# A chunked retention ahead of two MLPs: state matmuls on quarters of the array, query scaling on GpSimd, and an earlier second weight fetch

## Chip, cores and metric

The kernel runs on one core of a Trainium2 chip. The metric is the device time of one execution in microseconds. The trace is one profiled execution of the same kernel.

## The reference

For each batch b (2) and head h (8), over 768 positions of 64 features, a linear attention with a decay per head is computed, then two MLPs on the 1536 tokens of 512 features:

```python
for each block:                      # 64 positions in the reference
    intra = (q k^T * lam^(i-j), i>=j) v
    inter = (q * lam^(i+1)) @ state
    out   = intra + inter
    state = lam^block * state + (k * lam^(block-1-j))^T v
x = out as (tokens, heads*64)
x = relu(x @ w_in)^2 @ w_out         # 512 -> 2048 -> 512
y = leaky_relu(x @ w_in2) @ w_out2   # 512 -> 2048 -> 512
```

The weights come as float64, the rest as float32.

## The kernel before

**Retention.** The work is cut into 12 units (2 batches x 6 chunks of 128 positions), all 8 heads in one unit. A feature block of 128 partitions holds a pair of heads (p = 0 to 3), the even head in partitions 0 to 63 and the odd one in 64 to 127 (par = 0, 1). `load` (L196) fetches q, k or v of a unit, 256 KB each, on SP's queue. `transposes` (L288) turns k and q by TensorE (L294) and copies them out by ScalarE (L298). `scale_q` (L301) multiplies the transposed queries by the powers of lam, on VectorE, out of PSUM (L304). `scores` (L306) multiplies keys and queries, each head on one half of the array's rows (L311), and `mask` (L313) multiplies by the decay table (L316, VectorE). `state` (L323) scales k by GpSimd (`kd`, L329), multiplies it with v (L335), scales the old state by GpSimd (`tmp`, L342, once for each half of the partitions) and adds on VectorE (L347, or L349 in a chunk 0, twice also). The carried state `st` is a tile of 128 x 4 x 128 in which each pair's two 64 x 64 blocks stand on the diagonal and the rest is zero (L321), so that a state matmul reads 128 rows. `output` (L351) makes for each pair two state matmuls (L360, where the chunk isn't the first) and two score matmuls (L362) into one bank; `split` (L67) writes the result as a rounded part `xhi` (ScalarE, L68) and a rest `xlo` (VectorE, L69). A matmul in plain float32 stands in the trace as two MATMUL instructions, so 8 matmuls are x16.

**Order.** PE's and SP's orders in the retention are those of the program (`manual_schedule`, L414). In iteration i (L391 to L410) PE does transposes(i+2), state(i), output(i), scores(i+2), and SP issues k and q of unit i+4, v of unit i+2, and, for i = 1 and 9, a `fetch` of 1 MB of weights. VectorE, ScalarE and GpSimd work in the order that a planner gave them, except that the steps of a weight conversion in the retention are kept in program order (`pin`). k has 5 buffers, q and v 3 each, PSUM 8 banks.

**Weights.** `order` (L79) lists 32 pieces of 1 MB. `fetch` (L90) loads the next into one of two `raw` buffers; `converting` (L98) turns float64 words into a rounded and a rest part: one ScalarE pass (L114), then VectorE steps L115, L116, L118, L121, L122, L125 and, after a ScalarE copy (L135), L137. Each call of `convert` (L153) does one such step. After the step of L122 the raw tile isn't read again, and there a new fetch is made, but only if the MLP has begun:

```python
        yield ve.scalar_tensor_tensor(out=rf, in0=w_lo, ...)   # L122
        if begun_mlp:
            fetch()
```

In the retention `convert` is called once in each of the iterations 3 to 9, seven steps: the first piece.

**MLPs.** From L749 on PE's order is again the program's: first the halves of w_in against the three token tiles (first half of the first stage, then the second), then w_out, stage by stage; all MLP matmuls stand in line 503. One fetch is made at the start (L750), the others after L122.

## Time and profile before

| | us |
|---|---|
| median of 3 runs (lowest, highest) | 576.50 (575.89, 577.19) |
| the profiled execution | 576.09 |
| its span in the trace | 574.3 |
| TensorE busy in the span | 564.1 |
| VectorE busy | 418.9 |
| ScalarE busy | 304.4 |
| GpSimd busy | 90.7 |
| granted TensorE clock, share of full speed | 1.0 |

A row of a timeline gives start and length in us, the engine, the line, and the names of the tiles written and read; x4 means four instructions merged into one row; in brackets stand the idle time before it and what ended it. SPq is SP's queue of DMA issues: its time is the issuing, not the transfer. A group's row gives busy us, mean ns of one instruction, and the idle time before. PEld is TensorE's weight load.

### The profile page before, as it was taken

To read this page: it belongs to the slowest core of one execution; us is meant where nothing else is said; L and a number is where in the kernel's file an instruction comes from. 1 tells how busy PE (TensorE), PEld (TensorE's weight loads), DVE (VectorE), ACT (ScalarE), POOL (GpSimd) and SP (SyncE) were. 2 spreads that over 40 slices of the span, in tenths; PEclk is the share of its full clock that TensorE was granted. 3 is DMA by queue.
4 is the path that set the end of the run, shared out by engine and by line. 5 is a ranking of instruction groups with operands and counts; after the bars stand their busy time and mean duration, and the time that the engine had idled before them with its cause. 6 is when DMAs were issued, how large, how long until landed. Compare 5 with 4: busy or idle time off the path is not lost.

```text
span 574.3 us, 8060 instructions
## 1 busy us (share of the span) xinstructions
PE 564.1 (98%) x3075; PEld 470.4 (82%) x3075; DVE 418.9 (73%) x589; ACT 304.4 (53%) x477; POOL 90.7 (16%) x105
## 2 busy tenths in 40 slices
PE   7989999999999999999999999999999999999997
PEld 6879888888788888888888888888888888888886
DVE  3789999999927699498478999929883996217222
ACT  2344598547757587758447375453562376225110
POOL 3426000000044604343000000000213011310000
PEclk9999999999999999999999999999999999999999
DMA  8998434655498958999313215342529523661432
GB/s 173 244 201 188 155 121 135 233 184 190 163 156 138 155 175 183 211 258 227 128 36 95 80 33 218 130 164 74 105 53 246 110 33 42 76 89 56 164 111 91
DMA packets 79350, 80.75 MB, mean 141 GB/s; under 512 B 40264, under 2 KB 51792, under 8 KB 79312
## 3 DMA queue, kind: packets, MB, share of 16 engines
q1 hardware_dynamic: 61312, 62.15, 35.5%
q0 software_dynamic: 17472, 17.83, 22.9%
q8 instruction: 24, 0.39, 0.3%
q10 hardware_dynamic: 528, 0.26, 0.2%
q14 instruction: 14, 0.11, 0.1%
HBM read 55.05 MB, written 30.42 MB: 149 GB/s over the span
## 4 chain that ended last, share of the span: by engine, by line
PE 75%; DVE 16%; DMA 5%; issue 3%; ACT 1%; DVEq 0%; SPq 0%; ACTq 0%
PE ps L503 72%; DVE hb L118 2%; DVE rb L122 2%; DVE hb L125 2%; DMA v<-in_v 2%; DVE Pm L316 1%; DVE rb L121 1%; DVE hb L115 1%; DMA raw<-in_moe_w_in 1%; DVE xlo L69 1%; DMA raw<-in_moe_w_out 1%; DMA DTr<-tab 1%; DVE w2l L137 1%; PE ps L360 1%; DVE st L347 1%
## 5 line engine op out<-in xcount | busy, mean ns | idle before, releaser
L503 PE MATMUL ps<-xhi,w1h 128*128 128x512 f32 x288 | 112.2, 389 | 0.0
L503 PE MATMUL ps<-xhi,w1l 128*128 128x512 f32 x288 | 112.0, 389 | 0.0
L503 PE MATMUL ps<-xlo,w1h 128*128 128x512 f32 x288 | 112.0, 389 | 0.0
L616 POOL DMA_DIRECT2D spill<-f x48 | 47.9, 1215 | 349.9 <-ACT f L612 349.8
L612 ACT COPY f<-ps 128x512 f32<-128x512 f32 x84 | 48.7, 585 | 71.7 <-PE ps L503 71.2
L503 PEld LDWEIGHTS ps<-xhi,w1h 128*128 128x128 f32 x288 | 54.1, 188 | 11.4 <-issue 0.2
L503 PEld LDWEIGHTS ps<-xhi,w1l 128*128 128x128 f32 x288 | 54.1, 188 | 11.3
L503 PEld LDWEIGHTS ps<-xlo,w1h 128*128 128x128 f32 x288 | 54.1, 188 | 11.2
L474 DVE TENSOR_TENSOR g0l<-f,g0h 128x512 fp32r<-128x512 f32 x52 | 35.1, 687 | 32.5 <-ACT f L470 20.9
L503 PE MATMUL ps<-w2l,g0h 128*128 128x512 f32 (+1 forms) x132 | 50.5, 383 | 0.0
L503 PE MATMUL ps<-w2h,g0l 128*128 128x512 f32 (+1 forms) x132 | 50.5, 383 | 0.0
L503 PE MATMUL ps<-w2h,g0h 128*128 128x512 f32 (+1 forms) x132 | 50.5, 383 | 0.0
L137 DVE TENSOR_TENSOR w2l<-hb,w2h 128x1024 fp32r<-128x1024 f32 x16 | 19.5, 1222 | 39.8 <-ACT w2h L135 39.8
L114 ACT ACTIVATE hb<-raw 128x1024 f32<-128x1024 f32 x32 | 36.8, 1148 | 20.5 <-DVE w2l L137 7.5
L503 PE MATMUL ps<-g0h,w2h 128*128 128x512 f32 x104 | 40.5, 389 | 0.0
L503 PE MATMUL ps<-g0l,w2h 128*128 128x512 f32 x104 | 40.5, 389 | 0.0
L503 PE MATMUL ps<-g0h,w2l 128*128 128x512 f32 x104 | 40.5, 389 | 0.0
L122 DVE SCALAR_TENSOR_TENSOR rb<-raw,rb 128x1024 f32<-128x1024 uint32 x32 | 39.1, 1221 | 0.4
L125 DVE TENSOR_TENSOR hb<-hb,rb 128x1024 f32<-128x1024 f32 x32 | 39.1, 1221 | 0.4
L118 DVE SCALAR_TENSOR_TENSOR hb<-raw,hb 128x1024 uint32<-128x1024 uint32 x32 | 39.1, 1221 | 0.3
L567 DVE TENSOR_TENSOR f<-ps,f 128x512 f32<-128x512 f32 x40 | 26.2, 684 | 9.9 <-PE ps L503 9.9
L716 DVE TENSOR_TENSOR f<-ps,f 128x512 f32<-128x512 f32 (+1 forms) x25 | 16.7, 668 | 22.8 <-PE ps L503 22.8
(143 smaller groups left out, 1141.9 us busy)
## 6 DMA issues: line engine op xcount, KB each, us to landing
raw<-in_moe_w_in SPq DMA_DIRECT2D x16, 1024.0 KB, 5.6
raw<-in_moe_w_out SPq DMA_DIRECT2D x16, 1024.0 KB, 5.2
spill<-f POOLq DMA_DIRECT2D x48, 256.0 KB, 6.1
spill<-f SPq DMA_DIRECT2D x24, 256.0 KB, 2.8
f<-spill SPq DMA_DIRECT2D x24, 256.0 KB, 2.9
k<-in_k SPq DMA_DIRECT2D x12, 256.0 KB, 4.7
q<-in_q SPq DMA_DIRECT2D x12, 256.0 KB, 5.2
v<-in_v SPq DMA_DIRECT2D x12, 256.0 KB, 4.9
```

What stands on the lines that cost most here:

```text
L69: nc.vector.tensor_tensor(out=lo, in0=src, in1=hi, op=ALU.subtract)
L114: nc.scalar.activation(hf, w_hi.bitcast(F32), AF.Abs)
L118: yield ve.scalar_tensor_tensor(out=hb, in0=w_hi, scalar=0xC0000000, in1=hb, op0=ALU.bitwise_and, op1=ALU.bitwise_or)
L122: yield ve.scalar_tensor_tensor(out=rf, in0=w_lo, scalar=2.0 ** -52, in1=rf, op0=ALU.mult, op1=ALU.mult)
L125: yield ve.tensor_tensor(out=hf, in0=hf, in1=rf, op=ALU.add)
L137: yield ve.tensor_tensor(out=lo, in0=hf, in1=hi, op=ALU.subtract)
L474: nc.vector.tensor_tensor(out=glo, in0=r, in1=ghi, op=ALU.subtract)
L503: nc.tensor.matmul(ps, a, b, start=start and n == 0, stop=stop and n == len(ops) - 1, skip_group_check=again)
L567: ve.tensor_tensor(out=out, in0=ps[h, where], in1=other, op=ALU.add)
L612: nc.scalar.copy(f, src)
L616: nc.gpsimd.dma_start(dst, f, accum_op=ALU.add)
L716: nc.vector.tensor_tensor(out=a, in0=ps, in1=a, op=ALU.add)
```

## The change

The state tile has 64 columns instead of 128, without the zero blocks, and the two halves of its update become one instruction each. A state matmul takes 64 rows and writes 64 partitions. For odd pairs p the two heads change places in the output's partitions, so that four successive state matmuls lie on the four quarters of the array; output takes two banks, even pairs in one and odd pairs in the other, and is split in two instructions of each kind. All state matmuls of a unit come before its score matmuls. Because the heads of odd pairs are swapped in x, the rows of the first MLP's w_in are swapped as they are fetched: such a fetch is three DMAs (512 KB, 256 KB, 256 KB). Query scaling goes to GpSimd, from the copied queries in SBUF. The second fetch is made in iteration 6 instead of 9, and `convert` is called once in the iterations 3 to 5 and twice in 6 to 10: 13 calls.

```diff
--- before.py
+++ after.py
@@ -76,6 +76,9 @@
             return w[:, s * FS + h * CW:s * FS + (h + 1) * CW].rearrange("(k p) f -> p k f", p=P)
         return w[s * FS + h * CW:s * FS + (h + 1) * CW, :].rearrange("(k p) f -> p k f", p=P)
 
+
+    half = [slice(e * D, (e + 1) * D) for e in range(2)]
+
     order = [(0, 0, 0, 0), (0, 0, 0, 1), (0, 0, 1, 0), (0, 0, 1, 1)]
     stages = [(l, s) for l in range(2) for s in range(NS)]
     for before, stage in zip(stages, stages[1:]):
@@ -92,7 +95,13 @@
             key = todo.pop(0)
             r = raw.tile([P, 4 * CW], I64, tag="raw", name="raw")
             k = 4 if key[2] == 0 else 2
-            dma(r.rearrange("p (k f) -> p k f", k=k), source(*key))
+            dst, src = r.rearrange("p (k f) -> p k f", k=k), source(*key)
+            if key[0] or key[2]:
+                dma(dst, src)
+            else:
+                dma(dst[:, 0:k:2], src[:, 0:k:2])
+                for a, b in ((half[0], half[1]), (half[1], half[0])):
+                    dma(dst[a, 1:k:2], src[b, 1:k:2])
             fetched.append((key, r))
 
     def converting():
@@ -301,7 +310,7 @@
         def scale_q(i, ps):
             if units[i][1]:
                 qS[i] = tr.tile([P, NP, C], F32, tag="qS", name="qS")
-                ve.tensor_tensor(out=qS[i], in0=ps, in1=LR, op=ALU.mult)
+                nc.gpsimd.tensor_tensor(out=qS[i], in0=qT[i], in1=LR, op=ALU.mult)
 
         def scores(i):
             raw_scores[i] = [bank().rearrange("p (a s) -> p a s", a=NP) for _ in range(2)]
@@ -317,8 +326,7 @@
 
         st = []
         for e in range(2):
-            st.append(att.tile([P, NP, P], F32, name=f"st{e}"))
-            nc.gpsimd.memset(st[e], 0.0)
+            st.append(att.tile([P, NP, D], F32, name=f"st{e}"))
 
         def state(n):
             b, c = units[n]
@@ -337,33 +345,32 @@
             old, new = st[c % 2], st[(c + 1) % 2]
             if c:
                 tmp = wk.tile([P, NP, D], F32, tag="tmp", name="tmp")
-                for par in range(2):
-                    r = slice(par * D, (par + 1) * D)
-                    nc.gpsimd.tensor_tensor(out=tmp[r], in0=old[r, :, r],
-                                            in1=LR[r, :, C - 1:C].to_broadcast([D, NP, D]), op=ALU.mult)
-            for par in range(2):
-                r = slice(par * D, (par + 1) * D)
-                if c:
-                    nc.vector.tensor_tensor(out=new[r, :, r], in0=ps[r], in1=tmp[r], op=ALU.add)
-                else:
-                    nc.vector.tensor_copy(new[r, :, r], ps[r])
+                nc.gpsimd.tensor_tensor(out=tmp, in0=old, in1=LR[:, :, C - 1:C].to_broadcast([P, NP, D]), op=ALU.mult)
+                nc.vector.tensor_tensor(out=new, in0=ps, in1=tmp, op=ALU.add)
+            else:
+                nc.vector.tensor_copy(new, ps)
 
         def output(n):
             b, c = units[n]
             vn = nats[n, "v"]
-            ps = bank().rearrange("p (a s) -> p a s", a=NP)
-            for p in range(NP):
-
-                rows = [slice(par * D, (par + 1) * D) for par in range(2)]
-                if c:
-                    for r in rows:
-                        nc.tensor.matmul(ps[r, p, :], st[c % 2][:, p, r], qS[n][:, p, :], start=True, stop=False)
-                for par, r in enumerate(rows):
-                    nc.tensor.matmul(ps[r, p, :], vn[:, 2 * p + par, :], Pm[n][:, par, p, :], start=c == 0, stop=True)
+            ps = [bank()[:, 0:2 * C].rearrange("p (a s) -> p a s", a=2) for _ in range(2)]
+            heads = [(p, par ^ p % 2) for p in range(NP) for par in range(2)]
+
+            def place(p, par):
+                return ps[p % 2][half[par ^ p % 2], p // 2, :]
+
+            if c:
+                for p, par in heads:
+                    nc.tensor.matmul(place(p, par), st[c % 2][half[par], p, :], qS[n][half[par], p, :],
+                                     start=p < 2, stop=False, skip_group_check=True)
+            for p, par in heads:
+                nc.tensor.matmul(place(p, par), vn[:, 2 * p + par, :], Pm[n][:, par, p, :],
+                                 start=c == 0, stop=True, skip_group_check=True)
             t, o = divmod(b * S + c * C, TT)
             if xhi[t] is None:
                 new_x(t)
-            split(xhi[t][:, :, o:o + C], xlo[t][:, :, o:o + C], ps)
+            for e in range(2):
+                split(xhi[t][:, e::2, o:o + C], xlo[t][:, e::2, o:o + C], ps[e])
 
         n_units = len(units)
         FILL = TT // C
@@ -395,7 +402,7 @@
                 load(i + 4, "kq")
             if i + 2 < n_units:
                 load(i + 2, "v")
-            if i in (1, 9):
+            if i in (1, 6):
                 fetch()
             if i:
                 if i > 1:
@@ -405,7 +412,7 @@
                     mask(i + 1)
                 if i + 2 < n_units:
                     scores(i + 2)
-            if 3 <= i <= 9:
+            for _ in range((3 <= i <= 10) + (6 <= i <= 10)):
                 convert(pin=True)
 
 
```

## Rows read from the trace of the kernel before

**Rows 1.** Windows: us, then PE, PEld, DVE, ACT, POOL busy, clock, DMA, GB/s.

```profile
34.64:63.75 29.11, 29.09 (x472) 26.03 (x473) 28.23 (x47) 12.68 (x22) 11.23 (x13) 1.00 0.86 210
63.75:574.30 510.55, 506.68 (x2245) 419.52 (x2244) 370.36 (x492) 279.31 (x436) 66.14 (x68) 1.00 0.55 132
```

**Rows 2.** Waits of PE from 64 us to the end, all of them.

```profile
PE ps L503 <- DVE g1l L69: 0.4, 1, 0.4
```

**Rows 3.** Timeline of PE, iteration 7.

```profile
45.72 0.66 PE L294 MATMUL ps<-ident,k 128*128 128x128 f32 x4
...
46.74 0.69 PE L335 MATMUL ps<-v,kd 128*64 128x64 f32 x16
47.25 0.39 PE L360 MATMUL ps<-qS,st 128*64 128x128 f32 x4
47.47 0.39 PE L362 MATMUL ps<-Pm,v 128*64 128x128 f32 x4
...
49.10 1.16 PE L311 MATMUL ps<-qT,kT 64*128 64x128 f32 x16
50.20 0.33 PE L294 MATMUL ps<-ident,k 128*128 128x128 f32 x1
```

**Rows 4.** Timeline of PE, iteration 9 to the MLP's first matmul.

```profile
55.70 0.69 PE L335 MATMUL ps<-v,kd 128*64 128x64 f32 x16
...
61.42 0.76 PE L360 MATMUL ps<-qS,st 128*64 128x128 f32 x3
...
63.75 0.50 PE L503 MATMUL ps<-xhi,w1h 128*128 128x512 f32 x1
```

**Rows 5.** Timeline of DVE, one iteration's round and the next one's start.

```profile
49.19 0.86 DVE L347 TENSOR_TENSOR st<-ps,tmp 64x256 f32<-64x256 f32 x2
...
51.89 1.22 DVE L125 TENSOR_TENSOR hb<-hb,rb 128x1024 f32<-128x1024 f32 x1
53.02 0.68 DVE L304 TENSOR_TENSOR qS<-ps,LR 128x512 f32<-128x512 f32 x1
53.62 0.86 DVE L347 TENSOR_TENSOR st<-ps,tmp 64x256 f32<-64x256 f32 x2
```

**Rows 6.** Timeline of POOL in the retention.

```profile
43.91 1.23 POOL L329 TENSOR_TENSOR kd<-k,kdec 128x512 f32<-128x512 f32 x1 [7.41 <-PE ps L335]
45.24 1.31 POOL L342 TENSOR_TENSOR tmp<-st,LR 64x256 f32<-64x256 f32 x2
52.05 1.95 POOL L329 TENSOR_TENSOR kd<-k,kdec 128x512 f32<-128x512 f32 x1 [1.07 <-issue]
```

**Rows 7.** Windows, the loading: columns as in rows 1.

```profile
25.00:35.00 10.00, 8.38 (x134) 7.36 (x132) 6.71 (x12) 4.07 (x7) 4.27 (x6) 1.00 0.91 233
35.00:45.00 10.00, 10.00 (x161) 8.91 (x159) 9.68 (x16) 3.76 (x8) 2.13 (x2) 1.00 1.07 209
45.00:55.00 10.00, 10.00 (x162) 8.96 (x160) 9.63 (x17) 4.59 (x8) 7.38 (x9) 1.00 0.75 164
```

**Rows 8.** Chain of waits: the v of unit 4.

```profile
25.30 9.20 DMA v<-in_v
```

**Rows 9.** Timeline of SP's issues: v of unit 8, then of units 9 to 11.

```profile
44.98 0.72 SPq L65 DMA_DIRECT2D v<-in_v  x1
...
48.14 5.92 SPq L65 DMA_DIRECT2D v<-in_v  x3
```

**Rows 10.** Tile v, the issue at 48.14 alone (v of unit 9).

```profile
DMA to landing us min/median/max: 5.1/5.1/5.1
```

**Rows 11.** Tile v, the issue at 44.98 alone (v of unit 8).

```profile
DMA to landing us min/median/max: 4.6/4.6/4.6
```

**Rows 12.** Tile raw, the issue at 54.11 alone (second weights).

```profile
DMA to landing us min/median/max: 5.7/5.7/5.7
```

**Rows 13.** Timeline of ACT around the first weights' landing.

```profile
30.11 1.14 ACT L114 ACTIVATE hb<-raw 128x1024 f32<-128x1024 f32 x1 [3.12 <-DMA raw<-in_moe_w_in]
...
31.62 0.59 ACT L298 COPY qT<-ps 128x512 f32<-128x512 f32 x1
```

## The prediction

> **What bounds the kernel now.** I read the windows first. From 63.75 us to the end TensorE is busy for nearly the whole stretch [rows 1], and the list of its waits there has one entry, 0.4 us [rows 2]. So the MLPs, 510.5 of 574.3 us, can give back no more than that; what the change can win lies ahead of 63.75.
>
> In the retention I read the timeline of PE. Iteration 7 runs from 45.72 to 50.20, 4.48 us, without a gap: transposes 1.02, state 0.51, output 1.85, scores 1.10 [rows 3]. VectorE is as full: its round takes 49.19 to 53.62, 4.43 us [rows 5], 28.2 of 29.1 us are busy [rows 1]. Third come the loads. The windows show the DMA engines at 233 and 209 GB/s [rows 7], and the chain of waits has unit 4's v, issued at 25.30 and landed at 34.50, just before the state matmul that opens the second window of [rows 1] at 34.64 [rows 8]. So up to there the loads set the time: whatever the change saves before 34.64 is hidden, as is what it adds there (GpSimd's scaling of the first units, the first fetch in three DMAs). After it TensorE sets the time, with VectorE close and the loads a little ahead: v of unit 9 is issued at 48.14 and lands 5.1 later, at 53.24 [rows 9, 10], and its matmul starts at 55.70 [rows 4], 2.5 us of slack.
>
> **The array.** A group of four L360 instructions (two heads) takes 0.22 [rows 3], so a unit's state matmuls are 4 x 0.22 = 0.88. On four quarters four heads run at once: 0.44 at best, and sixteen L335 instructions in 0.51 show that the engine can issue them about that fast; I take 0.45. The ends are 0.44 and 0.88, the latter if only two run at once. But the array's form now changes twice more in a unit (128 rows, 64 rows, 128 rows). What a change costs is read from the scores: sixteen L311 instructions take 1.10, where sixteen of 128 columns at the pace of L360 take 0.88, so 0.22 around one change. I take 0.15 for each of the two new ones, ends 0 and 0.22, since the excess also holds the larger weight loads. Output: 1.85 - 0.88 + 0.45 + 0.30 = 1.72, a gain of 0.13 a unit (ends: gain 0.44, loss 0.44). The seven outputs with a carried state after 34.64 (units 4, 5, 7 to 11) gain 0.9.
>
> Against this stands a case in which the quarters don't overlap. The two heads of a pair use different row halves and write the same bank; in the kernel before, L311 alone uses row halves at once, and there the two write different banks, so no row shows the other. Were such heads to exclude each other, the state matmuls would stay at 0.88 and an output would take 1.85 + 0.30 = 2.15. The Trainium skill says that different row tiles can't use one PSUM bank at the same time (TensorEngine Tiling (Array Packing), Gotcha 1: PSUM Pressure); by it a unit would lose 0.30 where the sum has a gain of 0.13.
>
> **VectorE.** Gone from its round: the scaling, 0.60 (53.02 to 53.62), and one of two adds, 0.43 [rows 5]. Added: the split in two halves, each at about the add's 0.43 (it too has 256 elements), some 0.15 together over the single one. 4.43 - 0.60 - 0.43 + 0.15 = 3.55 with one conversion step, at most 1.13 (51.89 to 53.02). With two steps, from iteration 6 on, at most 4.7, against 4.35 of TensorE. It falls behind by 0.3 a round at worst; the mask is made one unit ahead, which covers it. If that cover is gone (units 10 and 11), up to 1.3 over four rounds.
>
> **GpSimd and ScalarE.** Scaling is an operation of the shape of `kd`, 1.23, or 1.95 where it ran beside a VectorE step [rows 6]. With one `tmp` of 0.65 (half of 1.31) GpSimd has 1.23 + 1.23 + 0.65 = 3.1 a unit, 4.55 at worst. The scaled queries wait for ScalarE's copy, and `kd` and `tmp` stand behind them; but scaled queries are used two units later and `kd` is made a unit ahead, so I cost it at nothing, up to 0.2 a unit without that cover (4.55 - 4.35). ScalarE is busy for 12.7 of 29.1 us [rows 1], so a second copy per unit is free. Output holds two of the eight banks instead of one; a wait for a bank would be at most a half split, 0.43 a unit; TensorE shows no such wait in [rows 3], so I take nothing. The two cleared state tiles fall away ahead of 34.64: nothing.
>
> **The second fetch** moves from behind v of unit 11 to behind v of unit 8, ahead of k11, q11 and v9 on SP's queue. It is 1.05 MB in three DMAs; two more issues are hidden, since an issue already keeps SP for 0.7 to 2 us [rows 9], time in which it can fall behind only if the transfers don't set the pace. What it costs the loads behind it is worked out from the windows: 25 to 35 us moved 2.33 MB with the first weights in it; the other 1.28 MB at 209 GB/s take 6.1 us, so the weights took 3.9 [rows 7]. Above stands 5.7, issue to landing of 1 MB with little else on the way [rows 12]; below 1.4, if the piece first fills the idle quarter of 45 to 55 us, 2.5 [rows 7]. That quarter comes after v9's issue, so I take 3.9: v9 lands at 57.1. TensorE would be there at 55.70 - 4 x 0.13 = 55.2, so it now waits for v9, and state(9) starts at 57.3 (0.14 after landing, as for unit 4), 1.6 later than before. That is the change's new wait; behind it on TensorE stands all that is left of the retention.
>
> From state(9) to the first MLP matmul took 63.75 - 55.70 = 8.05 [rows 4]. Off go 3 x 0.13 = 0.4 and the stall at the last output, where three L360 take 0.76 instead of four taking 0.39, for a late state: 0.3, as the state's add is shorter (lower end 0). MLP start: 57.3 + 7.35 = 64.65, **0.9 later**.
>
> **In the MLPs** VectorE has six conversion steps fewer at the start, so the one wait of 0.4 [rows 2] should go (ends 0 and 0.4). A side effect: the step after which a fetch is made now falls into the retention, where none is made, so from then on one piece is on its way where there were two. From a fetch to the next: 5.7 to land [rows 12], 1.14 for ScalarE's pass [rows 13], five steps of at most 1.22 [rows 5]: 12.9, while a piece is wanted each 510.5 / 32 = 16 us [rows 1]. Cost: nothing, with 3 us to spare. The six later split fetches have an idle SP queue.
>
> **Sum.** 0.9 - 0.4 = +0.5 on the profiled 576.09 (span 574.3, 1.8 around it). That run lies 0.41 under the median of 576.50; on the median the forecast is 577.0. A measurement of this kernel tells about 0.2% (1.15 us) from no change, so this counts as the same.
>
> **Rivals.**
> 1. *The loads keep up.* The fetch fills idle DMA time, delays v9 by 1.4 to 54.64, and TensorE's own pace decides: start 63.75 - 7 x 0.13 - 0.3 = 62.55, with the MLP's 0.4 in all -1.6: 574.9; with free form changes v9 binds at 54.8, and then 54.8 + 8.05 - 3 x 0.43 - 0.3 = 61.25, in all -2.9: 573.6. For it: DMA share 0.75 in that window; against: it is over 0.9 in the two before [rows 7]. Chance 0.22.
> 2. *ScalarE stands in front.* At 30.11 the first weights' pass waited 3.12 for its landing with kT and qT queued behind it; qT was done at 32.21 [rows 13]. Again so: the second weights land at 49.6 + 3.9 = 53.5 (v8 landed at 44.98 + 4.6 [rows 9, 11]), qT is done at 55.6, then scores and transposes, 2.12, and state(9) at 57.8: 577.5; with 5.7 for the fetch 579.3. It decides once the landing is later than 53.1, and only if the pass is queued ahead of unit 10's copies. Chance 0.15.
> 3. *The quarters exclude each other* (above): slower. state(9) still waits for v9 (TensorE there at 56.9); then three outputs lose 0.3 each: 57.3 + 8.05 + 0.9 - 0.3 = 65.95, in all +1.8: 578.3. It needs only that two heads of one bank don't overlap. Chance 0.12.
> 4. *The weights come late.* With one piece on its way instead of two, VectorE's other work must stretch the 12.9 by over 3 us; then TensorE waits in the first stages, 2 us or so: 579. Chance 0.06.
>
> **Numbers.** The forecast has 0.45, with its own range 575.5 to 578.4 (fetch 3.2 to 5.2, the ends of the array's and the stall's terms). Faster by over 0.2% (under 575.35): 0.18 from rival 1, 0.04 from the forecast, 0.22. Slower (over 577.65): 0.08 + 0.07 + 0.11 + 0.04 = 0.30. The same: 0.48. The range takes in most of rivals 1 to 3: 574.7 to 579.0.
>
> **What would show it.** Right: TensorE waits for v or for k and q of units 9 to 11, state(9) starts near 57, the MLP near 64.6, sixteen state matmuls within about 0.45, the entry of [rows 2] gone. Wrong: no DMA wait after 40 us and an MLP start before 63 (rival 1); a ScalarE pass waiting for raw near 50 with unit 10's copies behind it (2); state matmuls starting two at a time, 0.88 a unit (3); waits of PE for weights after 70 us (4).

## The result, and the profile after

| | forecast | measured |
|---|---|---|
| median, us | 577.0 (574.7 to 579.0) | 585.0 (582.96 to 586.51, 6 runs) |
| ratio to the kernel before (576.68, 6 runs) | | 1.0137, interval 1.0113 to 1.0161 |
| the profiled execution, its span | | 586.51, 584.7 |
| first MLP matmul | 64.65 | 64.88 |
| from it to the end (before 510.6) | 510.2 | 519.9 |

The change makes the kernel slower by 1.4%, outside the range. The profiled execution is the slowest of the six, 1.5 us over their median, so its 519.9 may hold that much more than a usual run. Lines after line 100 have moved: 114, 122 are now 123, 131; 304 is 313, 335 is 343, 347 is 349, 360 is 364, 503 is 510.

The windows, as in [rows 1]:

```profile
34.64:64.88 30.24, 27.91 (x466) 22.90 (x462) 27.29 (x43) 13.15 (x28) 16.54 (x13) 1.00 0.91 205
64.88:584.70 519.82, 509.48 (x2246) 420.50 (x2244) 369.26 (x491) 278.02 (x436) 65.50 (x68) 1.00 0.54 130
```

The waits of PE from 64 us on, where [rows 2] had one entry of 0.4:

```profile
PE ps L510 <- ACT g1h L68: 4.7, 2, 2.4
PE ps L510 <- DVE g0l L495: 1.3, 1, 1.3
PE ps L510 <- DVE g1l L69: 0.9, 2, 0.7
```

So 1.1 us were added ahead of the MLPs (forecast 0.9), and 9.3 inside them, where the forecast had a gain of 0.4. TensorE's holes lie at 152 to 160 us and at 222 to 226 us. The matmuls that end them, in the timeline of PE:

```profile
154.41 0.50 PE L510 MATMUL ps<-g0l,w2h 128*128 128x512 f32 x1 [1.29 <-DVE g0l L495]
...
159.62 0.50 PE L510 MATMUL ps<-g1h,sw 128*128 128x512 f32 x1 [2.42 <-ACT g1h L68]
...
225.28 0.49 PE L510 MATMUL ps<-g1h,sw 128*128 128x512 f32 x1 [2.27 <-ACT g1h L68]
226.44 0.50 PE L510 MATMUL ps<-g1l,sw 128*128 128x512 f32 x1 [0.66 <-DVE g1l L69]
```

TensorE waits for activations (g0, g1), not for weights. Both holes lie where a stage turns to w_out, the first in the second stage of the first MLP, the other in its third. g0l and g1l are written by VectorE, and ScalarE's copy g1h waits for VectorE too (the copy at 158.94 stood 1.56 us for the step of L498). What holds VectorE is in its own waits. First the kernel before, 34.64 to 155.1 us (the end of its one wait), then after, 34.64 to 160.3:

```profile
DVE sw L442 <- ACT sw L441: 1.1, 1, 1.1
DVE hb L115 <- ACT hb L114: 0.5, 1, 0.5
```

```profile
DVE hb L124 <- ACT hb L123: 5.4, 5, 1.8
DVE xlo L69 <- ACT xhi L68: 1.5, 2, 1.1
DVE sw L449 <- ACT sw L448: 1.1, 1, 1.1
```

The 5.4 are five conversions whose first VectorE step waits for ScalarE's pass, and that pass for the landing of the raw weights. The chain of waits of after shows the last of the five, whose fetch took 9.03 from issue to landing (its counterpart before 5.4, from 131.43 to 136.84). The timeline of DVE shows the last two waits, and the step at which the hole ends:

```profile
133.29 9.03 DMA raw<-in_moe_w_out
142.34 1.13 ACT hb L123
```

```profile
137.85 0.70 DVE L124 TENSOR_SCALAR hb<-hb 128x1024 f32<-128x1024 f32 x1 [1.06 <-ACT hb L123]
...
143.50 0.69 DVE L124 TENSOR_SCALAR hb<-hb 128x1024 f32<-128x1024 f32 x1 [1.76 <-ACT hb L123]
...
159.60 0.69 DVE L69 TENSOR_TENSOR g1l<-f,g1h 128x512 fp32r<-128x512 f32 x1 [0.35 <-ACT g1h L68]
```

VectorE works in order, so what stands behind the step at 143.50, the activations of the second stage among it, comes that much later. The windows from the first MLP matmul to the end of the first hole close the account; before first, then after:

```profile
63.75:155.10 91.35, 90.98 (x401) 75.00 (x400) 89.09 (x113) 63.91 (x96) 0.00 (x0) 1.00 0.49 161
```

```profile
64.88:160.30 95.42, 91.53 (x402) 74.92 (x400) 87.62 (x112) 60.85 (x93) 0.00 (x0) 1.00 0.49 155
```

The third figure is VectorE. Before it was busy for 89.1 of 91.35 us, idle for 2.3: the stretch in which TensorE seemed to set the time had two engines with hardly any slack. After it does 1.5 us less work but idles for 7.8, so the hole ends 4.1 us later after the MLP's start. The other 5 us are the second hole, 3.4, and a stretch behind it in which TensorE runs at half clock:

```profile
227.30:230.70 3.40, 3.40 (x10) 2.62 (x9) 3.40 (x6) 2.40 (x6) 0.86 (x1) 0.51 0.85 194
```

The second hole has the same cause, one stage on. The timelines of SP, ACT and DVE in after:

```profile
205.17 1.87 SPq L65 DMA_DIRECT2D raw<-in_moe_w_in  x3
216.17 1.12 ACT L123 ACTIVATE hb<-raw 128x1024 f32<-128x1024 f32 x1 [4.98 <-DMA raw<-in_moe_w_in]
217.32 0.69 DVE L124 TENSOR_SCALAR hb<-hb 128x1024 f32<-128x1024 f32 x1 [3.91 <-ACT hb L123]
```

Before, this piece was fetched at 199.84 and VectorE waited for it for 0.97. In after the fetch left when the step of L131 had freed its buffer (203.89 + 1.22 = 205.11): a VectorE that is late makes its next landing late.

### The profile page after: what moved, and what is told of

Its sections match the earlier page's. It is cut to its first block, busy times and chain, and to the rows that moved or that the text cites. A ratio compares the mean times of both kernels' runs of the same rounds, so it can differ in the third digit from the quotient of the medians.

```text
span 584.7 us, 8093 instructions
## 1 busy us (share of the span) xinstructions
PE 567.8 (97%) x3075; PEld 469.9 (80%) x3075; DVE 413.2 (71%) x581; ACT 304.4 (52%) x489; POOL 98.6 (17%) x105
## 4 chain that ended last, share of the span: by engine, by line
PE 74%; DMA 12%; DVE 7%; ACT 3%; issue 2%; SPq 1%; POOL 1%; DVEq 0%; ACTq 0%; POOLq 0%
PE ps L510 68%; DMA raw<-in_moe_w_out 5%; DMA raw<-in_moe_w_in 5%; PE ps L303 2%; ACT hb L123 2%; DMA v<-in_v 1%; DMA k<-in_k 1%; DVE rb L131 1%; PE ps L320 1%; PE ps L367 1%; SPq L65 1%; PE ps L343 1%; DVE rb L130 1%; DVE hb L134 1%; DVE hb L127 1%
## 5 line engine op out<-in xcount | busy, mean ns | idle before, releaser
L510 PE MATMUL ps<-xhi,w1h 128*128 128x512 f32 x288 | 112.1, 389 | 0.0
L510 PE MATMUL ps<-xlo,w1h 128*128 128x512 f32 x288 | 112.0, 389 | 0.0
L510 PE MATMUL ps<-xhi,w1l 128*128 128x512 f32 x288 | 112.0, 389 | 0.0
L510 PEld LDWEIGHTS ps<-xhi,w1h 128*128 128x128 f32 x288 | 54.1, 188 | 11.3 <-PE ps L367 0.2
L510 PEld LDWEIGHTS ps<-xhi,w1l 128*128 128x128 f32 x288 | 54.1, 188 | 11.2
L510 PEld LDWEIGHTS ps<-xlo,w1h 128*128 128x128 f32 x288 | 54.1, 188 | 11.2
L510 PE MATMUL ps<-w2l,g0h 128*128 128x512 f32 (+1 forms) x132 | 50.5, 383 | 0.0
L510 PE MATMUL ps<-w2h,g0l 128*128 128x512 f32 (+1 forms) x132 | 50.5, 383 | 0.0
L510 PE MATMUL ps<-w2h,g0h 128*128 128x512 f32 (+1 forms) x132 | 50.5, 383 | 0.0
L510 PE MATMUL ps<-g0l,w2h 128*128 128x512 f32 x104 | 40.8, 393 | 1.3 <-DVE g0l L495 1.3
L510 PE MATMUL ps<-g0h,w2h 128*128 128x512 f32 x104 | 40.8, 392 | 0.0
L510 PE MATMUL ps<-g0h,w2l 128*128 128x512 f32 x104 | 40.7, 392 | 0.0
L131 DVE SCALAR_TENSOR_TENSOR rb<-raw,rb 128x1024 f32<-128x1024 uint32 x32 | 39.6, 1238 | 0.4
L124 DVE TENSOR_SCALAR hb<-hb 128x1024 f32<-128x1024 f32 x32 | 22.4, 700 | 15.8 <-ACT hb L123 15.5
```

What stands on the lines that cost most here:

```text
L124: yield ve.tensor_scalar(out=hf, in0=hf, scalar1=2.0 ** -15, scalar2=122368.0, op0=ALU.max, op1=ALU.min)
L131: yield ve.scalar_tensor_tensor(out=rf, in0=w_lo, scalar=2.0 ** -52, in1=rf, op0=ALU.mult, op1=ALU.mult)
L510: nc.tensor.matmul(ps, a, b, start=start and n == 0, stop=stop and n == len(ops) - 1, skip_group_check=again)
```

## The experiments

Two theories were open at first: **P**, VectorE has no slack up to 155 us, and each landing that comes later than its order allows for passes through to TensorE; **L**, rival 4 of the prediction, only one piece of weights is on its way. The expectations use more letters: S, that the three DMAs of a w_in fetch land too late (a part of P); V, that VectorE is full up to some 155 us and TensorE loses what VectorE spends on late landings or on pieces not wanted yet; W, a rival of V, that a stage's own weights are late. They count the stages from 0. "MLP start" is the first MLP matmul of the profile, "MLPs" the time from it to the end. Since a single profile's loading varies (v of unit 4 is used at 34.2 in after and at 36.2 and 36.8 in two kernels that load the same), the starts compare to some 2 us. The MLPs' length isn't independent of the start: where VectorE sets the end of the first hole, a later start only makes the hole shorter. So the table at the end has that end too.

**e1_two_fetches**: after, with a second piece fetched where the MLP begins.

```diff
     fetch()
+    fetch()
```

> The changed kernel with two weight fetches at the start of the MLPs instead of one, so that two pieces are on their way again. Theory L (one piece on its way instead of two makes VectorE, which works in order, stand still for the weights' landing): VectorE's waits for ScalarE's pass between 64 and 155 us fall from 5.4 to under 1.5 us, the two holes of TensorE near 153 to 160 and 223 to 230 us go, the MLPs take about 511 us again instead of 520, and the time is 577 (576 to 578.5). Theory S (the three DMAs of a w_in fetch land too late): the holes stay, 583 to 586. If both count about alike: 580 to 581.

586.24 us, ratio 1.0175 (1.0159 to 1.0190): L's 577 missed. TensorE still loses 5.9 us in the MLPs, and VectorE waits 4.3 for landings. But counted from the MLP start, the fetches up to 150 us left at most 0.9 us earlier than in after: the second call puts hardly more on its way, so by itself this run doesn't try L.

**e2_one_dma**: after, each fetch of w_in in one DMA. It leaves out the swap of w_in's rows.

```diff
-            if key[0] or key[2]:
-                dma(dst, src)
-            else:
...
+            dma(dst, src)
```

> The changed kernel with each w_in fetch as one DMA of 1 MB again. This leaves out the swap of w_in's rows, so the first MLP multiplies swapped features by rows that aren't swapped; the amount of work is the same. Theory S: fetch to landing of w_in falls from 7 to 9 us to about 6, the holes of TensorE go, 577 to 578. Theory L: the holes stay, 583 to 585, with at most 1.5 us gained in the retention and a part of the holes.

579.6, ratio 1.0061 (1.0040 to 1.0083), between the two forecasts; the MLPs 513.96, 5.9 shorter than in after. More than half of the loss hangs on the three DMAs.

**e5_before_three_dmas**: the kernel before with w_in's fetches split the same way, rows unswapped.

```diff
-            dma(r.rearrange("p (k f) -> p k f", k=k), source(*key))
+            dst, src = r.rearrange("p (k f) -> p k f", k=k), source(*key)
+            if key[0] or key[2]:
+                dma(dst, src)
+            else:
+                dma(dst[:, 0:k:2], src[:, 0:k:2])
+                for a in (slice(0, D), slice(D, P)):
+                    dma(dst[a, 1:k:2], src[a, 1:k:2])
```

> The kernel before, with each w_in fetch of the first MLP as three DMAs (512, 256 and 256 KB) without a swap of rows, two pieces on their way. Theory L: no change, 576 to 577.5, since two pieces hide a later landing. Theory S: 582 to 586.

579.97, ratio 1.0065 (1.0050 to 1.0080): not L's "no change", and less than S had. The MLPs are 513.61, 3.0 longer than before. Its waits, of VectorE (64 to 165 us) and of TensorE (from 60 us):

```profile
DVE hb L121 <- ACT hb L120: 3.3, 2, 2.0
...
PE ps L509 <- DVE g1l L69: 2.0, 2, 1.3
PE ps L509 <- ACT g1h L68: 0.8, 1, 0.8
```

VectorE's waits for landings grow by 2.8, the MLPs by 3.0: the split alone does this, with nothing else of the change.

Why three DMAs come later is seen on SP's timeline (after):

```profile
118.63 0.38 SPq L65 DMA_DIRECT2D raw<-in_moe_w_in  x1
119.12 0.41 SPq L65 DMA_DIRECT2D spill<-f  x1
119.58 0.61 SPq L65 DMA_DIRECT2D raw<-in_moe_w_in  x1
120.27 0.55 SPq L65 DMA_DIRECT2D spill<-f  x1
120.88 0.61 SPq L65 DMA_DIRECT2D raw<-in_moe_w_in  x1
```

Between the issues of one piece stand issues of other data, so the last part leaves 2.25 us after the first. ScalarE's pass over this piece starts at 127.41, 8.8 after the first issue; its counterpart before was issued at 116.95 and passed from 123.20 on, 6.3. In e5, where the split is the only change, it is 7.8 (121.34 to 129.12), with the last part 2.55 behind the first. The Trainium skill advises that splitting DMAs can let the whole end sooner where the DMA engines are mostly idle (Perfetto Trace Analysis, DMA Optimizations). Here they were about half idle (0.49 in the window above) and the split piece came later.

**e4_before_one_less**: the kernel before, without the fetch that the second piece makes.

```diff
-        if begun_mlp:
+        if begun_mlp and key != order[1]:
```

> The kernel before, with the one fetch left out that the second piece's step makes, so that from then on one piece is on its way instead of two. Theory L: holes of TensorE in the first two or three stages as in the changed kernel, 582 to 586. Theory S: no change, 576 to 577.5.

576.1, ratio 1.0005 (0.9993 to 1.0017). The fetches did not move against the MLP start: in the MLPs the planner issues one as soon as its buffer is free, wherever the program makes it. So a call fewer takes no piece off its way, and with that L's premise is gone: in the changed kernel, too, the fetches go by free buffers.

**e6_hold** and **e7_before_hold**: after and before, with the conversion of w_in for the third and fourth stage held back until the second half of the stage ahead. This tries the last part of V, that pieces not wanted yet are converted ahead of this stage's activations.

```diff
+        if key in held:
+            return
...
+    held = {(0, s, 0, h) for s in (2, 3) for h in range(2)}
...
+        held.difference_update((0, s + 1, 0, h) for h in range(2))
```

> The changed kernel, in which the conversion of the next stage's w_in (two pieces, not needed before about 190 us, and the same one stage later) is held back until the stage's second half begins. Theory V (VectorE's queue is full until about 160 us and works in order; TensorE loses in the stages 1 and 2 what VectorE spends standing before a landing or on pieces that nobody wants yet): the holes near 153 to 160 and 223 to 230 us go, the MLPs take 511 to 512 us instead of 520, 576.5 to 578.5. Rival W (TensorE waits there because the stage's own weights are late): the holes stay, 583 to 586.

> The kernel before with the same holding back. Theory V: its one wait of TensorE near 154 us goes, 575.5 to 576.5. Rival W: no change, or slower where a held piece comes late, 576.5 to 579.

583.93, ratio 1.0136 (1.0120 to 1.0153), and 576.11, 0.9999 (0.9988 to 1.0010). V's 576.5 to 578.5 for e6 missed, but in neither did the held steps move; the planner put them ahead again, so they were pinned next. (The MLPs of e6 are 6 us shorter than in after, but they start 4 later: the first hole ends at 161.8, in after at 160.3, which makes 2.5 of the 6. The rest is mostly that e6's profile has no second hole; why is open.)

**e12_pinned_hold** and **e13_before_pinned_hold**: the same with the held pieces' steps kept in program order.

```diff
-            if pin:
+            if pin or key in late_keys:
```

> The changed kernel with the holding back of the next stage's two w_in pieces, this time with their first VectorE step pinned to its place in the program, since the planner moved the steps ahead again in the run without a pin (their L122 steps stood at the same times). Theory V: VectorE is relieved of about 13 us of work ahead of 155 us, the holes near 153 to 160 and 223 to 230 go, the MLPs take 511 to 512 us: 576.5 to 579. Rival W (own weights late): 583 to 586.

> The same holding back, pinned, in the kernel before. Theory V: the wait of 0.65 goes, 575.4 to 576.3; a loss only if a held piece comes late (over 577).

591.34, ratio 1.0250 (1.0220 to 1.0280), and 589.0, 1.0215 (1.0192 to 1.0239): both far over V's times. But the first hole is gone in both: from the MLP start TensorE doesn't wait once until 184 us in e12 and 182 in e13, though e12 has the quarters, GpSimd's scaling, the split and the early fetch. The window of e12:

```profile
65.17:155.00 89.83, 89.83 (x398) 74.41 (x397) 71.07 (x91) 62.49 (x97) 0.00 (x0) 1.00 0.41 129
```

VectorE is idle for 18.8 us there, where in after it was for 7.8 of 95.4. So the first hole does hang on VectorE's load, as V says. What V had wrong is the gain: the held pieces now come late themselves (in e13 ScalarE's pass at 185.58 stood 4.49 us for the landing of w_in), and new holes near 183 and 253 us in both cost more than the old ones.

**e9_late_convert** and **e10_all**: after with the second fetch in iteration 9 and seven conversion steps, as before; e10 has the hold of e6 also.

```diff
-            if i in (1, 6):
+            if i in (1, 9):
...
-            for _ in range((3 <= i <= 10) + (6 <= i <= 10)):
+            for _ in range(3 <= i <= 9):
```

> The changed kernel with the early conversion undone: the second fetch is made in iteration 9 again, and there is one call of convert in the iterations 3 to 9. The quarters, the scaling on GpSimd and the split fetches stay. If the second fetch is what delays the retention: no wait for v of unit 9, the MLPs begin at 61.5 to 63 instead of 64.9. Theory V: the MLPs keep the loss of the split fetches, 3 us or more, 514 to 520; in all 577 to 583.

> The last with the holding back too. Theory V: MLPs in 511 to 512 us from a start at 61.5 to 63, 574.3 to 576.5, which is under the kernel before. Rival W: 577 to 583, as without it.

579.4, ratio 1.0054 (1.0036 to 1.0072), and 578.53, 1.0044 (1.0018 to 1.0069). The MLPs of e9 are 514.47 (forecast 514 to 520), 5.4 shorter than in after: taking out the early conversion gives about as much as taking out the split. For e10 V's 574.3 to 576.5 missed: the MLPs start at 61.56, 2.2 earlier than before the change, but the first hole ends only 1.1 earlier than the kernel before's one wait, and the whole isn't faster.

**d1_before_more_vector**: the kernel before, with one more VectorE step in each of four pieces (it repeats line 115's), 2.8 us of work that the planner knows of.

```diff
+        if key in order[3:7]:
+            ve.tensor_scalar(out=hf, in0=hf, scalar1=2.0 ** -15, scalar2=122368.0, op0=ALU.max, op1=ALU.min)
```

> The kernel before, in which four pieces (the fourth to the seventh, converted between about 75 and 115 us) do the step of L115 twice; the second time it changes nothing. That adds 4 x 0.69 = 2.8 us to VectorE's queue and no landing, no DMA and no word of weights is late by more than that. Theory V: VectorE has no slack up to 155 us, so TensorE's wait near 154 us grows from 0.65 to about 3 us, 578.5 to 580. Rival: VectorE has slack and only late landings hurt: 576 to 577.

576.66, ratio 1.0008 (0.9994 to 1.0022); the MLPs 511.23, 0.7 longer. V's 578.5 to 580 missed, and its rival, that only late landings hurt, had 576 to 577. Up to 155.1 us VectorE is busy for 89.2 us, as before: work known to the planner is mostly moved out of the way. So the strict form of P, that each us of VectorE's passes through, falls; a wait for a landing that isn't in the plan does pass in e5.

**e14_before_early**: the kernel before with the early fetch and conversion alone.

```diff
-            if i in (1, 9):
+            if i in (1, 6):
...
-            if 3 <= i <= 9:
+            for _ in range((3 <= i <= 10) + (6 <= i <= 10)):
```

> The kernel before with the early conversion alone: second fetch in iteration 6, as one DMA, and 13 calls of convert. The second fetch delays v of unit 9 and VectorE has up to two steps more a round: MLP start at 65 to 66.5 instead of 63.75. In the MLPs, theory V with a shifted order of VectorE's queue: 3 us lost as in the changed kernel with one DMA, 580 to 582; if the 3 us there came from the quarters or from GpSimd's scaling instead: 577.5 to 579.

584.31, ratio 1.0125 (1.0098 to 1.0151), over both forecasts. The MLPs start at 69.66, 5.9 later, and are 3.3 longer. Its wait of TensorE in the retention's end:

```profile
PE ps L360 <- DVE st L347: 2.6, 1, 2.6
```

The last state's add stands behind conversion steps on VectorE (it starts at 65.47; in after, with one add, at 62.74). Behind that hole TensorE ran at half clock for 3.4 us, which cost some 1.7 (an estimate: half of it). Wait and clock are 4.3 of the 5.9.

**h1_before_third_raw** (control) and **h2_third_raw**: before and after, with three raw buffers, so that a fetch needs not wait for a free one; the room comes from the buffers of w_out.

```diff
-    raw = ctx.enter_context(tc.tile_pool(name="raw", bufs=2))
+    raw = ctx.enter_context(tc.tile_pool(name="raw", bufs=3))
...
-        bufs = 1 if n == 0 else 3
+        bufs = 1 if n == 0 else 2
```

> Control: the kernel before with three raw buffers instead of two, and two buffers instead of three for the converted w_out halves, which makes the room. Theory P: VectorE hardly waits for landings in the kernel before, so there is nothing to win; 575.5 to 578 if the missing w_out buffer costs nothing. Over 579 the room costs too much, and the next run must be read against this one.

> The changed kernel with the same buffers. Theory P: a fetch no longer waits for the last piece but one, VectorE's waits for ScalarE's pass between 64 and 155 us fall from 5.4 to under 2 us, and the MLPs lose 0 to 3 us to the control instead of 9: 577 to 580.5. Rival (the loss comes from another order of VectorE's work, not from landings): 583 to 586.

583.03, ratio 1.0091 (1.0058 to 1.0124), and 585.46, 1.0142 (1.0100 to 1.0183). Both missed their forecasts, since the room costs too much: both lose 5 to 6 us at 327 to 338, where TensorE now waits for a VectorE step (L716 in h1). From 64 to 320 us, TensorE's waits for an L510 or L503 operand are, in h2 first and then in h1:

```profile
PE ps L510 <- DVE g1l L69: 0.2, 1, 0.2
```

```profile
PE ps L503 <- DVE g1l L69: 0.7, 1, 0.7
```

In after they were 6.9, so here the holes of the change are gone. But VectorE still waits 2.7 for landings in h2 (forecast under 2), and the control shows that the smaller w_out pool has a part in it. Its waits of VectorE (64 to 155 us) and its window:

```profile
DVE hb L115 <- ACT hb L114: 2.4, 2, 1.2
```

```profile
64.06:155.00 90.94, 90.94 (x402) 75.32 (x402) 84.58 (x107) 64.22 (x95) 0.00 (x0) 1.00 0.46 152
```

The landing waits are 2.4 where before had 0.5, and up to 155 us TensorE doesn't wait: VectorE does less there and idles for 6.4. So in these runs a late landing costs TensorE time only where VectorE has no slack. How much of h2's gain is the third buffer isn't shown.

**g1_shift_late**: the heads put back in their places by split's copies instead of by w_in's fetches, each fetch one DMA, with e9's late conversion.

```diff
+            split(xhi[t][:, 0::2, o:o + C], xlo[t][:, 0::2, o:o + C], ps[0])
...
-                split(xhi[t][:, e::2, o:o + C], xlo[t][:, e::2, o:o + C], ps[e])
+                split(xhi[t][half[e], 1::2, o:o + C], xlo[t][half[e], 1::2, o:o + C], ps[1][half[1 - e]])
```

> The changed kernel without the swap of w_in's rows: the odd pairs' heads are put back to their places as the output is split, in two instructions of 64 partitions for the odd pairs' bank, and each w_in fetch is one DMA again; the early conversion is undone too (second fetch in iteration 9, one call of convert in 3 to 9). So it is the quarters and GpSimd's scaling alone. Theory P: MLPs as before, 510.6 to 511.5, from a start at 61.5 to 63: 574 to 576, under the kernel before. Rival: MLPs of 513 to 515 as in the other runs of the changed kernel, 577 to 580.

584.25, ratio 1.0123 (1.0085 to 1.0161): P's 574 to 576 missed, and the rival too. There are three instructions of each kind per unit where after has two, and the MLPs start at 66.57. They are also 4.6 longer than before, with 2.9 of landing waits, though neither the split fetch nor the early conversion is in: about 1.6 of it is half clock behind its hole, the rest these runs don't explain.

**g6_before_pool**: the kernel before with the scaling on GpSimd alone.

```diff
-                ve.tensor_tensor(out=qS[i], in0=ps, in1=LR, op=ALU.mult)
+                nc.gpsimd.tensor_tensor(out=qS[i], in0=qT[i], in1=LR, op=ALU.mult)
```

> The kernel before with the scaled queries by GpSimd alone. VectorE's round gets shorter by 0.6, TensorE's not. If TensorE sets the retention: MLP start within 0.5 of 63.75 and 576 to 577. If VectorE held TensorE at the end (the stall at the last output): up to 0.5 earlier. If GpSimd's queue puts the first scaling ahead of the first scaled keys, TensorE stands at 11 to 14 us as in the changed kernel, hidden by the load of unit 4.

576.32, ratio 0.9989 (0.9973 to 1.0005). The start is 62.85, 0.9 earlier, the MLPs 512.34, 1.8 longer: what the retention wins is given back.

**g8_before_pool_early**: e14 and g6 together (their two diffs).

> The kernel before with the scaling on GpSimd and with the early conversion, the first fetch of w_in in one DMA. Theory P (VectorE without slack, each addition passes through): the scaling takes the 16 scaling instructions off VectorE's retention rounds, so the early conversion finds room: the MLPs start at 64 to 66 us (with the early conversion alone 69.66), and their length is 2 to 4 us over the 510.6 of the kernel before; 578 to 582 us. Rival (the room comes from the quarters and the merged state, not from the scaling): the MLPs start at 68 to 70 us as with the early conversion alone, and 583 to 586 us.

586.33, ratio 1.0152 (1.0108 to 1.0195); start 69.40, MLPs 517.47. My expectation missed, and its rival had the start (68 to 70): taking the scaling off VectorE doesn't make room for the early conversion. TensorE's and VectorE's waits:

```profile
PE ps L360 <- DVE st L347: 1.9, 2, 1.1
...
DVE hb L115 <- ACT hb L114: 5.7, 3, 2.8
```

Up to 1.7 of its late start is a half-clock stretch from 33.4 to 36.8. The 5.7 of waits for landings show that they don't need a split fetch; e14, without the scaling either, has 3.7.

**q1_quarters**: the quarters and the merged state alone, with each fetch in one DMA. It leaves out the swap of w_in's rows.

```diff
-            if key[0] or key[2]:
...
+            dma(dst, src)
...
-                nc.gpsimd.tensor_tensor(out=qS[i], in0=qT[i], in1=LR, op=ALU.mult)
+                ve.tensor_tensor(out=qS[i], in0=ps, in1=LR, op=ALU.mult)
...
-            if i in (1, 6):
+            if i in (1, 9):
...
-            for _ in range((3 <= i <= 10) + (6 <= i <= 10)):
+            for _ in range(3 <= i <= 9):
```

> The quarters and the merged state alone: scaled queries on VectorE, the second piece fetched and converted where the kernel before does it, each fetch of w_in in one DMA; the swap of the rows of w_in is left out, so the output is not the reference's. Theory P: the parts that add work to the stretch up to 155 us are gone, so the MLPs start at 62 to 63.3 us (the cheaper output and the merged state) and are 1 to 4 us longer than in the kernel before, because the planner's order is another one; 575.5 to 579 us. Rival (the quarters themselves cost TensorE or VectorE time that the other runs hide): the MLPs start after 64 us or lose over 6 us; 581 us or more.

578.1 (575.67 to 581.75), ratio 1.0039 (1.0017 to 1.0060), as P had it. The profile's own time is 575.67, 2.4 under the median: start 61.49, 2.3 earlier than before, MLPs 512.39, 1.8 longer. So the quarters aren't the bulk of the loss; but their gain isn't kept, and by the medians they end 2.1 slower.

The runs, in order of what TensorE loses in the MLPs. "Lost" sums the distances of successive matmul starts over 0.3 us, less the 0.227 at which they follow each other at full clock; "hole ends" is where TensorE resumes after the first hole (before: its one wait); "landing" is VectorE's wait for the ScalarE pass over raw weights, 64 to 165 us.

| kernel | MLP start | MLPs | lost | hole ends | landing |
|---|---|---|---|---|---|
| before | 63.75 | 510.6 | 0.8 | 155.1 | 0.5 |
| e7 hold | 63.69 | 510.6 | 0.8 | 155.1 | 0.4 |
| e4 one fetch less | 63.18 | 510.7 | 0.8 | 154.6 | 0.5 |
| d1 more VectorE work | 63.51 | 511.2 | 1.3 | 155.1 | 0.6 |
| g6 scaling on GpSimd | 62.85 | 512.3 | 2.2 | 154.3 | 0.4 |
| q1 quarters alone | 61.49 | 512.4 | 2.6 | 154.6 | 1.0 |
| e5 split alone | 64.34 | 513.6 | 3.8 | 156.7 | 3.3 |
| e6 after, hold | 68.89 | 513.8 | 4.0 | 161.8 | 3.1 |
| e10 after, late, hold | 61.56 | 513.9 | 4.0 | 154.0 | 1.4 |
| e14 early alone | 69.66 | 513.9 | 4.1 | 161.6 | 3.7 |
| e2 after, one DMA | 63.69 | 514.0 | 4.1 | 156.7 | 3.0 |
| e9 after, late | 63.21 | 514.5 | 4.7 | 155.9 | 2.9 |
| g1 heads put back, late | 66.57 | 515.2 | 5.4 | 160.9 | 2.9 |
| e1 after, two fetches | 68.36 | 515.8 | 5.9 | 163.0 | 4.3 |
| g8 early and GpSimd | 69.40 | 517.5 | 7.2 | 164.5 | 5.7 |
| after | 64.88 | 519.9 | 9.9 | 160.3 | 5.4 |

The pinned holds (12.2 and 13.8 lost) and the third buffers are left out, since they lose later and for other reasons. Half clock behind a hole is some 1.6 of the lost time in after, e1, e6 and g1, some 3 in g8. Little is lost where the landing waits are short, most where they are longest, though not in step: g6 and e10 lose 2.2 and 4.0 with 0.4 and 1.4 of landing waits. And the hole's end hardly follows the start: from 61.5 to 64.3 us of start it moves between 154.0 and 156.7, and is latest in e2 and e5, which have the longest landing waits of these. No kernel beats the one before beyond the noise of the measurement.

## Why the prediction was wrong

**The retention was right.** State and output of an iteration, timeline of PE in after, beside [rows 3]:

```profile
45.93 0.69 PE L343 MATMUL ps<-v,kd 128*64 128x64 f32 x16
46.54 0.67 PE L364 MATMUL ps<-qS,st 64*64 64x128 f32 x16
47.14 1.09 PE L367 MATMUL ps<-Pm,v 128*64 128x128 f32 x16
48.17 1.16 PE L320 MATMUL ps<-qT,kT 64*128 64x128 f32 x16
49.26 0.66 PE L303 MATMUL ps<-ident,k 128*128 128x128 f32 x4
```

From 45.93 to 48.17 are 2.24, where before took 2.36: a gain of 0.12 a unit for a forecast of 0.13. Sixteen state matmuls end within 0.67 of the first's start, so four run at once and rival 3 falls. The two heads of a pair here use different row halves and one bank; the rule of the Trainium skill that different row tiles can't use one PSUM bank at the same time (TensorEngine Tiling (Array Packing), Gotcha 1: PSUM Pressure) is not what this trace shows. The form changes cost 0.10 (state 0.61 for 0.51) and 0.20 (0.60 from the first state matmul to the first score matmul, 0.40 of it the matmuls), for 0.15 each.

**The new wait came where it was put**, as in [rows 4]:

```profile
52.27 0.65 PE L364 MATMUL ps<-qS,st 64*64 64x128 f32 x12 [0.93 <-DVE xlo L69]
...
55.71 0.63 PE L303 MATMUL ps<-ident,k 128*128 128x128 f32 x4 [0.68 <-DMA k<-in_k]
56.73 0.63 PE L303 MATMUL ps<-ident,q 128*128 128x128 f32 x4 [0.39 <-DMA q<-in_q]
57.69 0.69 PE L343 MATMUL ps<-v,kd 128*64 128x64 f32 x16 [0.33 <-DMA v<-in_v]
...
64.88 0.50 PE L510 MATMUL ps<-xhi,w1h 128*128 128x512 f32 x1
```

k and q of unit 11 and v of unit 9 land late behind the early fetch; state(9) starts at 57.69 for 57.3, and 7.19 later, for 7.35, the MLPs. So rival 1 falls, and rival 2 wasn't needed. That 64.88 came so close to 64.65 is in part luck: e1, e6 and e12 have the same retention and start their MLPs at 68.36, 68.89 and 65.17. How the loss splits is therefore that of one profile: in e6 5.1 us of it lie ahead of the MLPs and 3.2 inside, where the forecast still had a gain. One price was wrong and hidden: the wait for a bank, costed at nothing, is the 0.93 at 52.27 (for VectorE's part of the split), ahead of the waits for loads. GpSimd's scaling took 2.26 in two units, over the upper bound of 1.95, and was covered too, but for 2.3 at the start, hidden behind the loads.

**The step that failed is the one on the MLPs**: that "VectorE has six conversion steps fewer at the start, so the one wait of 0.4 [rows 2] should go", with "Cost: nothing, with 3 us to spare" for the fetches. Two things in it were wrong. First, the bound: the prediction read from [rows 1] and [rows 2] that TensorE sets the time from 63.75 on. That bounds what a change can win there, not what it can lose. [rows 1] give one figure for VectorE there, 370 of 511 us, and its parts weren't looked at: in the first 91 us it is busy for 89. There 2.8 us more of waits for landings made the MLPs 3.0 longer (e5), and six steps fewer are no gain when the next ones wait for data. Second, the spare time: a piece each "510.5 / 32 = 16 us" is the mean over the whole stretch. At its start the planner's order takes the pieces faster; ScalarE's passes over the first and the tenth of them in after:

```profile
62.76 1.18 ACT L123 ACTIVATE hb<-raw 128x1024 f32<-128x1024 f32 x1 [2.28 <-DMA raw<-in_moe_w_out]
142.34 1.12 ACT L123 ACTIVATE hb<-raw 128x1024 f32<-128x1024 f32 x1 [2.70 <-DMA raw<-in_moe_w_out]
```

That is one each 8.8 us (before, from 63.24 to 136.87, one each 8.2): against it the 12.9 from fetch to fetch leaves no 3 us to spare. (Fetches overlap there: one left at 133.29, while the piece fetched at 127.30 was passed over at 136.70.) What counts is each landing against the place of its first step in VectorE's fixed order. The split moves the landings back: alone it costs 3.6 us in all (579.97 for 576.36 on the same chip, 3.0 of it in the MLPs). The early conversion moves the fetches themselves and puts conversion steps ahead of the last state's add: alone it costs 7.9 (584.31 for 576.37, 5.9 in the retention). Together that is 11.5, more than the 8.3 by which after is slower by the medians (10.4 by the profiles): both lose at the same two places (e5's holes end at 156.7 and 221.3, e14's at 161.6 and 226.9), and taken out of after one by one (e2, e9) they give back 5.4 and 5.6. About 1.6 of the profile's loss is the half clock behind the second hole.

Rival 4 had the right place, late data in the first stages, but not the mechanism: the "one piece on its way instead of two" didn't come about, since neither one fetch more nor one fewer in the program moves the fetches of the MLPs (e1, e4), and TensorE waited for activations, not for weights.

**What stays open.** The parts don't add up: each edit also gives the planner's order another form. g6's MLPs are 1.8 longer without a wait for a landing, g1's 4.6 without either of the two causes, and how much of each loss is such an order can't be told apart with these runs. The third buffer has its own side effect. And what in after lets the MLPs start at 64.88, where e14 and g8 have over 69, wasn't tried by itself: the nearest is the merged add, whose last one the planner put ahead of a conversion step, where e14's stands behind two.

## What to carry to other kernels

Before you call an engine the bound of a long stretch, look at the other engines' busy time in its parts: a second engine that is full for the first 91 of 510 us decides there, and the bound's list of waits doesn't show it. An engine without slack that works in a fixed order pays in full for a landing that comes later than that order allows for, while work that the planner knows of is mostly absorbed; so cost a change to a DMA (its split, its place, what stands between its issues) by the first instruction that waits for it, not by mean rates. And a gain in front of such a stretch is kept only if the second engine also gets ahead.

## What the runs showed of the hardware

The granted clock of TensorE fell to half (1.2 GHz) at places that the prediction had none for. In after, one such stretch began within a TensorE wait of 2.30 us that ended at 13.86, and one behind the waits that ended at 225.28 and 226.44; the kernel before, with 1.90 at the same early place, kept full clock there. The early stretch of after:

```profile
12.30:19.10 6.80, 5.24 (x50) 4.61 (x52) 3.67 (x7) 1.75 (x4) 2.73 (x3) 0.50 1.05 210
```

Matmuls of 512 columns then start 0.427 apart instead of 0.227, so 3.4 us of it cost 1.6. A short wait can thus be paid for twice: e14's of 2.63 us, in a stretch that was full otherwise, was followed by 3.4 us at half clock. The early stretch is hidden by the loads: v of unit 4 is used at 34.23 in after, at 34.64 before.
